# A planned kernel of retention and a two-layer PReLU network: scores and states of a pair of heads in one piece, and a planner that counts array switches and holds loads back

## The chip, the cores and the metric

The kernel runs on one NeuronCore of a Trainium2 chip: TensorE (PE) multiplies matrices, VectorE (DVE), ScalarE (ACT) and GpSimd (POOL) work elementwise, SyncE (SP) and ACT issue DMAs. Each engine runs its own instructions strictly in order and waits on semaphores for the others. The metric is the device time of one execution in microseconds (us), the median of several runs.

## The reference

Eight batches of eight heads, 576 positions, head size 64, all fp32. Each head computes a causal decayed product; the heads of a position are joined to a row of 512, and 4608 rows go through a layer of 2048 with a per-column PReLU and back to 512:

```python
scores = scale * np.matmul(q, k.transpose(0, 1, 3, 2))
gamma = 1.0 - 2.0 ** (-5.0 - np.arange(H, dtype=np.float32))
Dmat = np.where(rel >= 0, gamma[:, None, None] ** rel[None, :, :], 0.0)
attn = np.matmul(scores * Dmat, v)
x = attn.transpose(0, 2, 1, 3).reshape(B * S, H * D)
h = x @ w_in
out = (np.maximum(h, 0.0) + alpha * np.minimum(h, 0.0)) @ w_out
```

## The kernel before

**The retention.** The 64 heads are taken as 32 pairs (two heads of 64 rows fill 128 partitions). A sequence is cut into nine chunks of 64 positions. Within a chunk the masked scores are computed directly; across chunks a 64x64 state per head is carried, decayed and added to. Pairs 0 to 3 (the first batch) are done by separate functions at the start. For each later pair, `joint(n)` (it does one pair's scores and states and the values of the pair before) records:
- the values of pair n-1 (`values`, matmuls on line 758, 128x64 weights, 18 of them in two pieces, into the two PSUM banks psh), and ACT's copies of them to x (line 773);
- the corner scores of the ninth chunk (line 796, 2 matmuls of 64x64 weights into a corner of psh1);
- the scores of eight chunks (line 804, 16 matmuls of 64x64) and the states' increments (line 813, 16 of 64x64), in the two banks psa;
- DMAs of the scaled q to the tile at; masks of the scores (DVE lines 842 and 849; for pairs 4 to 7, called FIRST, ACT line 827 and POOL line 833);
- the running sum of the states (ACT 855 and 865, DVE 860, 868 and 871) and its DMAs into the tile vn, from which the next pair's values are computed.

Ahead of it `load_kq` loads q and k in a layout for transposing (tiles qx and kx, four DMAs of 72 KB each in packets of 128 bytes; each tile exists once) and k as it stands (kn, two DMAs of 144 KB in packets of 256 bytes). `operands` scales qx on POOL (line 730), transposes both on DVE (line 737, to kT and qT) and scales kn on ACT (line 742). `load_v` loads v. Pairs in FIRST load qx and kn from ACT's queue, all others from SP's.

The trace counts each of these fp32 matmuls twice (36, 4, 32 and 32 for a pair).

**The network.** 144 cells, each a block of 256 rows by a unit of 256 hidden columns. The first eight cells use fp32 matmuls (lines 951 and 981). The other 136 split each number into pieces: 24 matmuls of 128x256 on line 1015 into psh0 and psh1, an elementwise chain on ACT and DVE (lines 1023 to 1030), the split of the result on ACT and POOL (lines 1039 to 1046), and, two cells later, 12 matmuls of 128x512 on line 1064. Weights are loaded as raw words, converted (ACT 640 and 642, DVE 650 to 661, POOL 664) and split (ACT 688, POOL 689, DVE 692); half of them are kept in DRAM (wk) and read back. Finished x blocks and partial outputs are kept in DRAM too (xk, ok).

**What sets the order.** `do` (line 191) records each operation with an engine, a cost, and what it reads and writes. `plan` (line 224) first walks backwards to give every operation a due time (`due`, counted back from the end), then forwards: on each engine, among the ready operations that could begin within `SLACK` of the earliest one, the one with the smallest due time is next. A DMA occupies one model wire for size / `RATE`, and may be issued at most `BACKLOG` = 2 us ahead of that wire. The operations are then emitted in this order. No time of the plan is kept in the program: it is only the order that the plan decides.

Of the kernel before, what the change touches and what calls it, by code (L numbers as in the profile page):

```python
# [21 lines left out]
def kernel(  # L22
# [17 lines left out]
    C = 64  # L40
# [5 lines left out]
    TB = 2 * P  # L46
# [71 lines left out]
    for i in range(NBIT - 1):  # L118
# [8 lines left out]
                            op=ALU.mult)  # L127
# [60 lines left out]
                self.tile = self.slot.make()  # L188
            return self.tile

    def do(eng, cost, fn, r=(), w=(), late=0.0, lock=False):
        deps, gens = set(), []
        for keys, writes in ((r, False), (w, True)):
            for g, *sub in keys:
                wr, rd = g.keys.setdefault(tuple(sub), ([], []))
                deps.update(wr)
                if writes:
                    deps.update(rd)
                deps.update(g.before)
                if g not in gens:  # L200
                    gens.append(g)
        op = Op(eng, cost, fn, None, [g.slot for g in gens if g.slot and g.slot.bank], late, lock)
        for g, *sub in w:
            g.keys[tuple(sub)] = ([op], [])
        for g, *sub in r:
            g.keys[tuple(sub)][1].append(op)
        for g in gens:
            assert not g.slot or g.slot.gen is g
            g.ops.append(op)
        op.deps = [d for d in deps if d is not op]  # L210
        op.gens = gens
        ops.append(op)
        return op


    RATE = 220e3

    def dma(to, fro, size, r, w, eng="SP"):
        queue = {"SP": nc.sync, "ACT": nc.scalar}[eng]
        do(eng, 0.56, lambda: queue.dma_start(to(), fro()), r, w, late=size / RATE)  # L220

    LAT = {"PE": 0.2}

    def plan():

        users = [[] for _ in ops]
        for op in ops:
            for d in op.deps:
                users[d.n].append(op)

        def wait(d, op):
            return 2.0 if d.late else 0.0 if d.eng == op.eng else LAT.get(d.eng, 0.1)


        due = [0.0] * len(ops)
        left = [len(users[op.n]) for op in ops]
        can = [0.0] * len(ops)
        free = {e: 0.0 for e in BEGIN}
        ready = {e: [] for e in BEGIN}
        for op in ops:  # L240
            if not left[op.n]:
                ready[op.eng].append(op)
        for _ in ops:
            pick = None
            for e, queue in ready.items():
                if queue:
                    t0 = min(max(free[e], can[op.n]) for op in queue)
                    op = max((op for op in queue if max(free[e], can[op.n]) <= t0 + 0.02),
                             key=lambda op: op.n)
                    t = max(free[e], can[op.n])  # L250
                    if pick is None or t < pick[0]:
                        pick = t, op
            t, op = pick
            ready[op.eng].remove(op)
            free[op.eng] = t + op.cost
            due[op.n] = -(t + op.cost)
            for d in op.deps:
                left[d.n] -= 1
                can[d.n] = max(can[d.n], t + op.cost + wait(d, op) + d.late)
                if not left[d.n]:  # L260
                    ready[d.eng].append(d)
        left = [len(op.deps) for op in ops]
        ready = {e: [] for e in BEGIN}
        rest = [op.n for op in ops if op.eng == "PE"]
        end, begin, order = [0.0] * len(ops), [0.0] * len(ops), []
        free, held, port, wire = dict(BEGIN), {}, [0.0, ""], 0.0
        can = [0.0] * len(ops)
        for op in ops:
            if not op.deps:
                ready[op.eng].append(op)  # L270

        def earliest(op):
            t = max(free[op.eng], can[op.n])
            for b in op.banks:
                if b in held:
                    t = max(t, max([x + LAT.get(e, 0.1) for e, x in held[b].items()
                                    if e != op.eng] or [0.0]))
            if op.lock and port[1] != op.eng:
                t = max(t, port[0])
            if op.late:  # L280
                t = max(t, wire - BACKLOG)
            return t

        while len(order) < len(ops):
            pick = None
            for e, queue in ready.items():
                if not queue:
                    continue
                c = [(earliest(op), op) for op in queue
                     if e != "PE" or op.n <= rest[0] + AHEAD_PE]  # L290
                if not c:
                    continue
                t0 = min(t for t, _ in c)
                t, op = min((x for x in c if x[0] <= t0 + SLACK.get(e, 0.05)),
                            key=lambda x: (due[x[1].n], x[1].n))
                if pick is None or t < pick[0]:
                    pick = t, op
            t, op = pick
            ready[op.eng].remove(op)
            if op.eng == "PE":  # L300
                rest.remove(op.n)
            begin[op.n] = t
            free[op.eng] = t + op.cost
            end[op.n] = t + op.cost
            if op.late:
                wire = max(wire, t + op.cost) + op.late
                end[op.n] = wire
            for b in op.banks:
                held.setdefault(b, {})[op.eng] = t + op.cost
            if op.lock:  # L310
                if port[1] == op.eng or t + op.cost > port[0]:
                    port[:] = [t + op.cost, op.eng]
            order.append(op)
            for u in users[op.n]:
                left[u.n] -= 1
                can[u.n] = max(can[u.n], end[op.n] + wait(op, u))
                if not left[u.n]:
                    ready[u.eng].append(u)
        total = max(end)
        return total, order, begin, end  # L320

    AHEAD_PE = 150
    BACKLOG = 2.0
    LAG, FIRST = 2, range(4, 8)
    SLACK = {"PE": 0.02}
    BEGIN = {"PE": 5.0, "ACT": 0.5, "DVE": 8.2, "POOL": 5.8, "SP": 0.5}


# [368 lines left out]
    pairs = [(b, c) for b in range(B) for c in range(NPAIR)]  # L697
    loaded, turned, mts = {}, {}, {}
# [18 lines left out]
    def load_v(n):  # L717
        b, c = pairs[n]
        for h2 in range(2):
            dma(lambda h2=h2: vns[n % 2][half(1 - h2), h2],  # L720
                lambda h2=h2: v[b, 2 * c + h2].rearrange("(j t) d -> t j d", t=C), S * D * 4, (),
                [(vnm[n % 2], "v", h2)])
# [25 lines left out]
    def values(n, pv):  # L748
        b, c = pairs[n]
        vn, mt = loaded[n][3], mts[n]  # L750
        w = TB // C
        j1 = -b * NJ % w or w
        j1 += w if NJ - j1 > 6 else 0
        for i, js in enumerate((range(0, j1), range(j1, NJ))):
            def f(i=i, js=js):
                for j in js:
                    for h2 in range(2):
                        nc.tensor.matmul(pv[i].get()[half(h2), (j - js[0]) * C:(j - js[0] + 1) * C],  # L758
                                         vns[n % 2][:, h2, j], mt.get()[:, h2, j], start=True,
                                         stop=True)  # L760
            do("PE", 0.14 * len(js), f,
               [(vn, x, h2) for x in "vs" for h2 in range(2)] + [(mt, x, h2) for h2 in range(2)
                                                                for x in ("q", 0, 1, "x")],
               [(pv[i], 0)])
        j = 0
        while j < NJ:
            kb, o = divmod(b * NJ + j, w)
# [7 lines left out]
            do("ACT", 0.12 + 0.065 * m, f, [(pv[i], 0)], [(xb[kb], "c", c, j)])  # L775
            j += m

    def joint(n):
        pv = [Gen(psh[m]) for m in range(2)]
        if n - 1 in mts:  # L780
            values(n - 1, pv)
            if n + 1 < len(pairs):
                load_v(n + 1)
        if n == len(pairs):
            return
        c = pairs[n][1]
        kT, qT = turned[n]
# [6 lines left out]
        def f():  # L794
            for h2 in range(2):
                nc.tensor.matmul(pv[1].get()[half(1 - h2), 7 * C:], kT.get()[half(h2), chunk(NJ - 1)],
                                 qT.get()[half(h2), chunk(NJ - 1)], start=True, stop=True)
        do("PE", 0.15, f, [(kT, 0), (qT, 0)], [(pv[1], "x")])

        def f():  # L800
            for j in range(NJ - 1):
                for h2 in range(2):
# [1 line left out]
                    nc.tensor.matmul(at(j % 2)[x, 0, j // 2], kT.get()[half(h2), chunk(j)],  # L804
                                     qT.get()[half(h2), chunk(j)], start=True, stop=True,
                                     skip_group_check=True)
        do("PE", 0.65, f, [(kT, 0), (qT, 0)], [(ps[0], 0), (ps[1], 0)])

        def f():
            for j in range(NJ - 1):  # L810
                for h2 in range(2):
# [1 line left out]
                    nc.tensor.matmul(at(j % 2)[x, 1, j // 2], kn.get()[half(1 - h2), j],  # L813
                                     vns[n % 2][half(1 - h2), h2, j], start=True, stop=True,
                                     skip_group_check=True)
        do("PE", 0.65, f, [(kn, 0), (kn, 1), (vn, "v", 0), (vn, "v", 1)], [(ps[0], 1), (ps[1], 1)])
        mt = mts[n] = Gen(ats)
        for h2 in range(2):
            dma(lambda h2=h2: mt.get()[half(h2), h2].rearrange("p j s -> p (j s)"),
# [450 lines left out]
```

## Time and profile before

| | before |
|---|---|
| runs | median 979.19 us (978.96 to 982.37, 6 runs) |
| profiled execution | 979.08 us, span 977.4 us |
| granted TensorE clock, mean | 0.988 |
| a 128x256 group of a cell, L1015 x24 | 2.87 us |
| a 128x512 group of a cell, L1064 x12 | 2.75 us |
| L758, L804, L813, L796 busy | 40.1, 20.2, 19.5, 9.1 us |
| DMA | 134.93 MB, 255053 packets, 218448 under 512 B |
| kx, qx (SP), qx (ACT), kn (SP), kn (ACT): issue to landing, median | 3.2, 2.9, 6.0, 3.6, 5.2 us |

The profile is one execution, some 1.7 us longer than its span. Its views are: a page with the busy share of each engine, in all and in 40 slices; the same by stages given in us, with the granted clock and the DMA share; the chain of work that ended last, followed back through what released each step; and the instructions of an engine in order of time, where a bracket tells how long the engine had been idle and what ended that. Matmuls are pipelined, so durations of single ones overlap; what counts is the distance from start to start.

### The profile page before, as it was taken

How to read it: one execution, taken by the hardware profiler on the slowest of the kernel's cores; microseconds unless marked ns; L12 is line 12 of the kernel's file. 1: busy time of each engine (PE TensorE's matmuls, PEld its weight loads, DVE VectorE, ACT ScalarE, POOL GpSimd, SP SyncE). 2: the span in 40 equal slices, each digit the busy share in tenths (PEclk: the TensorE clock that was granted, in tenths of full speed). 3: DMA queues.
4: the chain of work that ended last, by engine and by line, in shares of the span. 5: the costliest groups of instructions: out<-in, count | busy, mean ns of one | idle time of the engine just before them, and what ended most of it. 6: DMA issues, size and time to landing. Idle time of an engine off the chain costs nothing.

```text
span 977.4 us, 22758 instructions
## 1 busy us (share of the span) xinstructions
PE 937.8 (96%) x8713; PEld 821.5 (84%) x8713; DVE 616.2 (63%) x1294; ACT 583.8 (60%) x1313; POOL 637.1 (65%) x515
## 2 busy tenths in 40 slices
PE   4897789999999999999999999999999999999998
PEld 4665468888998888888889899999999999999996
DVE  5776766778666777787667777554554445444444
ACT  3575455757666657576678676665555555555542
POOL 3766665766775848567688889765555555665553
PEclk9899899999999999999999999999999999999999
DMA  9989787888665979887533536242122212121111
GB/s 235 201 169 225 141 197 161 204 183 202 178 142 135 209 148 216 187 211 190 175 130 130 172 103 186 91 150 66 65 76 72 91 65 66 67 86 44 44 45 65
DMA packets 255053, 134.93 MB, mean 138 GB/s; under 512 B 218448, under 2 KB 218464, under 8 KB 254944
## 3 DMA queue, kind: packets, MB, share of 16 engines
q1 hardware_dynamic: 238624, 130.59, 52.0%
q10 hardware_dynamic: 16320, 2.89, 2.0%
q8 instruction: 68, 1.11, 0.5%
q14 instruction: 41, 0.34, 0.1%
HBM read 82.19 MB, written 35.65 MB: 121 GB/s over the span
## 4 chain that ended last, share of the span: by engine, by line
PE 83%; DMA 7%; SPq 3%; DVE 2%; POOL 2%; ACT 1%; issue 1%; ACTq 0%; POOLq 0%; DVEq 0%
PE psh L1015 38%; PE pso L1064 36%; PE psh L758 3%; SPq L220 3%; DMA vn<-su 2%; PE psh L951 1%; PE psa L804 1%; DMA kn<-in_k_dram 1%; PE psa L813 1%; PE pso L981 1%; DMA at<-qT 1%; DMA w<-in_q_dram 1%; DMA kx<-in_k_dram 1%; DMA qx<-in_q_dram 1%; DMA w<-in_k_dram 1%
## 5 line engine op out<-in xcount | busy, mean ns | idle before, releaser
L1015 PEld LDWEIGHTS psh<-lx,w 128*128 128x128 f32 x3264 | 409.6, 191 | 13.9 <-DVE ga L1030 2.0
L1015 PE MATMUL psh<-lx,w 128*128 128x256 f32 x3264 | 419.0, 284 | 0.2
L1064 PE MATMUL pso<-w,g 128*128 128x512 f32 x1632 | 402.9, 393 | 1.0 <-POOL g L1046 1.0
L1064 PEld LDWEIGHTS pso<-w,g 128*128 128x128 f32 x1632 | 295.8, 188 | 58.0 <-POOL g L1046 2.1
L1043 POOL TENSOR_TENSOR g<-ga,g 128x512 fp32r<-128x512 f32 x136 | 180.0, 1324 | 232.7 <-ACT g L1039 232.4
L1024 DVE SCALAR_TENSOR_TENSOR ga<-psh,gt 128x256 f32<-128x256 f32 x272 | 114.5, 422 | 172.8 <-ACT gt L1023 167.3
L1046 POOL TENSOR_TENSOR g<-g 128x512 fp32r<-128x512 f32 x136 | 178.5, 1313 | 12.0 <-ACT g L1041 2.0
L1030 DVE SCALAR_TENSOR_TENSOR ga<-psh,malpha,ga 128x256 f32<-128x256 f32 x272 | 130.2, 480 | 68.0 <-ACT psh L1027 66.9
L1039 ACT ACTIVATE g<-ga 128x512 fp32r<-128x512 f32 x136 | 85.9, 631 | 121.2 <-PE pso L1064 104.3
L1027 ACT ACTIVATE psh<-ga 128x256 f32<-128x256 f32 x272 | 105.2, 388 | 88.4 <-DVE ga L1024 87.0
L1023 ACT COPY gt<-psh 128x256 f32<-128x256 f32 x272 | 101.0, 371 | 66.5 <-PE psh L1015 58.9
L934 POOL TENSOR_TENSOR lx<-lx 128x512 fp32r<-128x512 f32 x78 | 102.3, 1322 | 18.8 <-DVE lx L924 16.2
L1041 ACT ACTIVATE g<-ga 128x512 fp32r<-128x512 f32 x136 | 84.4, 620 | 0.0
L842 DVE SCALAR_TENSOR_TENSOR at<-psa,pf,mask 64x256 f32<-64x256 f32 x96 | 46.3, 483 | 17.8 <-PE psh L758 7.0
L758 PEld LDWEIGHTS psh<-at,vn 128*64 128x64 f32 x1008 | 34.9, 143 | 20.5 <-issue 13.0
L730 POOL TENSOR_TENSOR qx<-qx,tabx 128x576 f32<-128x576 f32 x28 | 32.4, 1158 | 28.7 <-DMA qx<-in_q_dram 19.8
L758 PE MATMUL psh<-at,vn 128*64 128x64 f32 x1008 | 40.1, 232 | 10.9 <-DVE ga L962 7.0
L917 ACT ACTIVATE lx<-x 128x512 fp32r<-128x512 f32 x78 | 48.7, 628 | 0.0
L931 POOL TENSOR_TENSOR lx<-x,lx 128x512 fp32r<-128x512 f32 x30 | 38.8, 1294 | 3.7 <-ACT lx L929 3.7
L1082 DVE TENSOR_TENSOR op<-pso,op 128x512 f32<-128x512 f32 x46 | 31.6, 686 | 14.2 <-PE pso L1064 14.2
L773 ACT COPY x<-psh 128x256 f32<-128x256 f32 (+3 forms) x84 | 23.7, 320 | 18.3 <-PE psh L758 12.2
L924 DVE TENSOR_TENSOR lx<-x,psa 128x512 fp32r<-128x512 f32 x48 | 32.6, 679 | 2.1 <-PE psh L1015 1.9
(173 smaller groups left out, 848.7 us busy)
## 6 DMA issues: line engine op xcount, KB each, us to landing
ok<-o SPq DMA_DIRECT2D x48, 256.0 KB, 2.9
op<-ok SPq DMA_DIRECT2D x24, 512.0 KB, 3.9
x<-xk SPq DMA_DIRECT2D x23, 512.0 KB, 3.4
xk<-x SPq DMA_DIRECT2D x18, 512.0 KB, 4.8
out_dram<-o SPq DMA_DIRECT2D x36, 256.0 KB, 2.4
kx<-in_k_dram SPq DMA_DIRECT2D x112, 72.0 KB, 3.2
vn<-in_v_dram SPq DMA_DIRECT2D x56, 144.0 KB, 3.4
at<-qT SPq DMA_DIRECT2D x56, 144.0 KB, 3.3
```

What stands on the lines that cost most here:

```text
L758: nc.tensor.matmul(pv[i].get()[half(h2), (j - js[0]) * C:(j - js[0] + 1) * C], vns[n % 2][:, h2, j], mt.get()[:, h2, j], start=True, stop= ...
L934: do("POOL", 1.29, lambda c=c: nc.gpsimd.tensor_tensor(out=piece(to.get()[:, 2, c]), in0=to.get()[:, 0, c], in1=to.get()[:, 1, c], op=ALU. ...
L1015: nc.tensor.matmul(at(b), piece(w[:, l, c0:c0 + P]), piece(x.get()[:, l, cc]), start=(n == 0 and cc == 0), stop=(n > 0 and cc == NCC - 1), ...
L1023: do("ACT", 0.36, lambda t=t, at=at: nc.scalar.copy(t(), at(1)), [(ph, 1)], [(gt, f)])
L1024: do("DVE", 0.42, lambda t=t, g=g, at=at: nc.vector.scalar_tensor_tensor(out=g(), in0=at(0), scalar=ONE, in1=t(), op0=ALU.mult, op1=ALU.su ...
L1027: do("ACT", 0.39, lambda g=g, at=at: nc.scalar.activation(at(1), g(), ACTF.Relu, scale=-1.0), [(ga, f)], [(ph, 1)])
L1030: do("DVE", 0.48, lambda g=g, at=at, fc=fc: nc.vector.scalar_tensor_tensor(out=g(), in0=at(1), scalar=malpha[:, fc:fc + 1], in1=g(), op0=A ...
L1039: do("ACT", 0.64, lambda: nc.scalar.mul(piece(to.get()[:, 2]), ga.get(), BELOW), both, [(to, 2)])
L1041: do("ACT", 0.64, lambda: nc.scalar.mul(piece(to.get()[:, 0]), ga.get(), BELOW * 2.0 ** -12), both, [(to, 0)])
L1043: do("POOL", 1.29, lambda: nc.gpsimd.tensor_tensor(out=piece(to.get()[:, 1]), in0=ga.get(), in1=to.get()[:, 2], op=ALU.subtract), both + [ ...
L1046: do("POOL", 1.29, lambda: nc.gpsimd.tensor_tensor(out=piece(to.get()[:, 2]), in0=to.get()[:, 0], in1=to.get()[:, 1], op=ALU.subtract), [( ...
L1064: nc.tensor.matmul(a[2 * m + b].get(), piece(g.get()[:, l, f, m * P:(m + 1) * P]), piece(w_at[u, 2 + f].get()[:, l]), start=(cell["first"] ...
```

## The change

1. The four pieces of a pair on PE (values in two, corner, scores, states) are first collected. Pairs 8 and later record corner and scores as one operation; FIRST pairs keep them apart. The operations of the joint are recorded values first, and the copies of the values and the next `load_v` after them.
2. An operation can have a kind. Scores, states and corner have the kind "half" on PE, all else the kind of its engine; where the kind differs from the last operation's, the forward walk counts 0.12 us more. PE's SLACK goes from 0.02 to 0.14. The costs of the pieces are set lower (0.65 to 0.47, 0.15 to 0.03, 0.14 to 0.133 a chunk).
3. RATE goes from 220 to 236 (KB/ms, that is GB/s). RATE_256 and RATE_128 are defined and `dma` takes a rate.
4. A DMA isn't planned earlier than `HOLD` = 30 us ahead of its due time.

```diff
-    def do(eng, cost, fn, r=(), w=(), late=0.0, lock=False):
+    def do(eng, cost, fn, r=(), w=(), late=0.0, lock=False, kind=None):
...
-        op.gens = gens
+        op.gens, op.kind = gens, kind or eng
...
-    RATE = 220e3
-
-    def dma(to, fro, size, r, w, eng="SP"):
+    RATE, RATE_256, RATE_128 = 236e3, 175e3, 115e3
+
+    def dma(to, fro, size, r, w, eng="SP", rate=RATE):
         queue = {"SP": nc.sync, "ACT": nc.scalar}[eng]
-        do(eng, 0.56, lambda: queue.dma_start(to(), fro()), r, w, late=size / RATE)
+        do(eng, 0.56, lambda: queue.dma_start(to(), fro()), r, w, late=size / rate)
...
+        last = -min(due)
...
             if op.late:
-                t = max(t, wire - BACKLOG)
-            return t
+                t = max(t, wire - BACKLOG, due[op.n] + last - HOLD)
+            return t + SWITCH.get(op.eng, 0.0) * (kinds[op.eng] != op.kind)
...
-    BACKLOG = 2.0
+    BACKLOG, HOLD = 2.0, 30.0
     LAG, FIRST = 2, range(4, 8)
-    SLACK = {"PE": 0.02}
+    GROUPS = (("v0",), ("v1",), ("x", "s"), ("u",))
+    SLACK, SWITCH = {"PE": 0.14}, {"PE": 0.12}
...
+    def on_pe(parts, groups):
+        for some in groups:
+            do("PE", sum(parts[x][0] for x in some), lambda some=some: [parts[x][1]() for x in some],
+               [key for x in some for key in parts[x][2]],
+               [key for x in some for key in parts[x][3]], kind="half" if not {"v0", "v1"} & set(some) else None)
...
     def joint(n):
         pv = [Gen(psh[m]) for m in range(2)]
+        parts = {}
         if n - 1 in mts:
-            values(n - 1, pv)
-            if n + 1 < len(pairs):
-                load_v(n + 1)
+            (parts["v0"], parts["v1"]), rest = values(n - 1, pv)
         if n == len(pairs):
+            on_pe(parts, [["v0"], ["v1"]])
+            rest()
             return
...
-        do("PE", 0.15, f, [(kT, 0), (qT, 0)], [(pv[1], "x")])
+        parts["x"] = 0.03, f, [(kT, 0), (qT, 0)], [(pv[1], "x")]
...
+        groups = [["v0"], ["v1"], ["x"], ["s"], ["u"]] if n in FIRST else GROUPS
+        on_pe(parts, [[x for x in some if x in parts] for some in groups])
+        if n - 1 in mts:
+            rest()
+            if n + 1 < len(pairs):
+                load_v(n + 1)
```

More of the change, by code (lines that the diff above doesn't have):

```diff
@@ L265, in plan @@
         end, begin, order = [0.0] * len(ops), [0.0] * len(ops), []
-        free, held, port, wire = dict(BEGIN), {}, [0.0, ""], 0.0
+        free, held, port, wire, kinds = dict(BEGIN), {}, [0.0, ""], 0.0, {e: e for e in BEGIN}
         can = [0.0] * len(ops)
@@ L302, in plan @@
             begin[op.n] = t
-            free[op.eng] = t + op.cost
-            end[op.n] = t + op.cost
+            kinds[op.eng] = op.kind
+            free[op.eng] = end[op.n] = t + op.cost
             if op.late:
@@ L753, in values @@
         j1 += w if NJ - j1 > 6 else 0
+        parts = []
         for i, js in enumerate((range(0, j1), range(j1, NJ))):
@@ L760, in f, with keep_x @@
                                          stop=True)
[L761 to L764, printed above, removed]
+            parts.append((0.133 * len(js), f, [(vn, x, h2) for x in "vs" for h2 in range(2)] +
+                          [(mt, x, h2) for h2 in range(2) for x in ("q", 0, 1, "x")],
+                          [(pv[i], 0)]))
+        return parts, lambda: keep_x(n, pv, j1)
+    def keep_x(n, pv, j1):
+        b, c = pairs[n]
+        w = TB // C
         j = 0
@@ L806, in f @@
                                      skip_group_check=True)
-        do("PE", 0.65, f, [(kT, 0), (qT, 0)], [(ps[0], 0), (ps[1], 0)])
+        parts["s"] = 0.47, f, [(kT, 0), (qT, 0)], [(ps[0], 0), (ps[1], 0)]
         def f():
@@ L815, in f @@
                                      skip_group_check=True)
-        do("PE", 0.65, f, [(kn, 0), (kn, 1), (vn, "v", 0), (vn, "v", 1)], [(ps[0], 1), (ps[1], 1)])
+        parts["u"] = (0.47, f, [(kn, 0), (kn, 1), (vn, "v", 0), (vn, "v", 1)],
+                      [(ps[0], 1), (ps[1], 1)])
+        groups = [["v0"], ["v1"], ["x"], ["s"], ["u"]] if n in FIRST else GROUPS
[4 more added lines that the diff above has]
+                load_v(n + 1)
         mt = mts[n] = Gen(ats)
```

## The prediction

> **What bounds the kernel now.** I read the page's busy table and its 40 slices first, then the stages of 25 us, then the chain of work that ended last, then the engine timelines of the first 150 us. The page:
>
> ```profile
> PE 937.8 (96%) x8713; PEld 821.5 (84%) x8713; DVE 616.2 (63%) x1294; ACT 583.8 (60%) x1313; POOL 637.1 (65%) x515
> ...
> PE   4897789999999999999999999999999999999998
> ...
> DMA  9989787888665979887533536242122212121111
> ```
>
> TensorE is the bound from slice 7 on, and the DMA engines are full in the first four slices. The stages (columns: us, busy PE, PEld, DVE, ACT, POOL, granted clock, DMA share, GB/s) say the same with numbers:
>
> ```profile
> 0.00:25.00 25.00, 12.10 (x309) 10.31 (x310) 14.66 (x56) 9.01 (x14) 10.12 (x23) 0.94 1.08 235
> 75.00:100.00 25.00, 19.22 (x250) 13.20 (x248) 15.64 (x28) 13.18 (x29) 16.98 (x18) 0.93 1.01 208
> 100.00:125.00 25.00, 17.41 (x234) 12.30 (x236) 16.70 (x33) 10.86 (x24) 14.56 (x14) 0.86 0.74 148
> 125.00:150.00 25.00, 21.11 (x266) 17.51 (x259) 17.43 (x41) 12.81 (x32) 16.75 (x14) 0.93 0.88 210
> 250.00:275.00 25.00, 25.00 (x254) 22.35 (x255) 14.89 (x34) 16.42 (x38) 19.89 (x17) 1.00 0.60 138
> ```
>
> So two places can give time: the start-up to about 146 us, with some 33 us of idle PE, and the stage to 480 us, where PE never idles but interleaves the pairs' small matmuls with the full ones. After 480 us only full matmuls are left (2.87 + 2.75 us a cell), in an unchanged order: nothing to gain.
>
> What a small piece costs is read in the chain of work that ended last (start, us, what). First a joint cut in pieces, then one whose pieces stand together:
>
> ```profile
> 191.03 2.75 PE pso L1064 x12
> 193.77 0.62 PE psa L813 x32
> 194.40 0.10 PE psh L796 x4
> 194.50 1.59 PE pso L1064 x6
> 196.09 1.20 PE psh L758 x36
> 197.29 1.58 PE pso L1064 x6
> 198.88 2.87 PE psh L1015 x24
> 201.75 1.39 PE pso L1064 x6
> ```
>
> ```profile
> 255.38 1.20 PE psh L758 x36
> 256.58 0.20 PE psh L796 x2
> ...
> 257.30 0.47 PE psa L813 x32
> 257.77 3.06 PE psh L1015 x24
> ```
>
> Prices: going back to full matmuls costs 0.19 (1.58 or 1.59 against 1.39, 3.06 against 2.87), after values (L758) as after scores or states. Going in with scores or states costs 0.15 (0.62 against 0.47 when other small ones stand before). Going in with values is free (1.20 behind full and small alike). Values to the corner piece L796 costs 0.16 (0.26 in all, behind L813 only 0.10).
>
> **The change, part by part.** (1) Joining and the switch count. I counted, in the two built programs' PE order from the first split cell on, the runs of small matmuls between full ones. Before: 42 runs, 24 that begin with scores, states or corner, 20 steps from values to these. After: 40 runs, 13, and 24 (thirteen are now values, corner, scores, with or without states). So before 42 x 0.19 + 24 x 0.15 + 20 x 0.16 = 14.8 us, after 40 x 0.19 + 13 x 0.15 + 24 x 0.16 = 13.4: **-1.4 us**, all on the path, since PE never idles there. Bounds: the runs of before took 18.5 us in the chain above their bare work (1.20 + 0.10 + 0.47 + 0.47 a joint), 0.45 each. Two runs less at 0.45 are 0.9; and if the 18 of the 40 that hold values, corner and scores cost 0.34 (2.39 from 255.38 to 257.77, + 0.19 - 2.24) and the other 22 cost 0.45, 16.0 are left, a gain of 2.5.
>
> The Trainium skill, TensorEngine Tiling (Array Packing), Key Properties, says that any change of tiling mode drains the array. The 128x64 values would then be a mode of their own, which the planner's two kinds leave out; the row speaks against half of that, since entering values costs nothing. By the rule all 114 changes before and 108 after cost the same, and this term would be 6 x 0.19 = -1.1 instead.
>
> (2) The rates. No call passes RATE_256 or RATE_128: small packets aren't counted, and every transfer is counted faster than before (220 to 236 GB/s; 72 KB from 0.33 to 0.31 us). On the chip such loads take 2.9 us (SP) or 6.0 us (ACT) from issue to landing (median). It acts only through the order, so its price is in (3) and (4).
>
> (3) HOLD in the first 40 us. Before, ACT issues ahead of its first L688 (37.08 us) the four qx and two kn loads of pair 4 and two qx loads of pair 5: 6 x 72 + 2 x 144 = 720 KB. After, three qx loads stand ahead of it: 216 KB. That is 504 KB less while the DMA engines are full; at 213 GB/s, between the stages 0 to 25 (235) and 25 to 50 (192), it is 2.4 us. What it now holds up:
>
> ```profile
> 2.73 4.56 ACTq L220 DMA_DIRECT2D qx<-in_q_dram  x3
> 20.89 1.15 POOL L730 TENSOR_TENSOR qx<-qx,tabx 128x576 f32<-128x576 f32 x1 [8.91 <-DMA kn<-in_k_dram]
> ```
>
> ACT stands 4.56 us in three issues ahead of its first copy, and POOL's in-order queue stands 8.91 us at qx while the first weight piece (DVE done at 19.06) waits behind it to 21.99. Only 0.5 of that is PE's: its next need, ACT's x, ends at 22.82, PE starts at 23.33. The chain runs through DMA here (q 1.93 to 8.80, weights 8.82 to 13.66, k 29.88 to 35.60), so most of the 2.4 is on the path. I take **-1.9 us** (0 to -2.9, the 2.4 and the 0.5; nothing in this stage is moved ahead, so no loss).
>
> (4) The four joints of the start-up (60 to 146 us). PE idles there for 0.9 + 3.8 + 1.0 + 7.0 + 0.5 + 0.2 + 2.0 + 1.9 = 17 us. Three things change. Stores (ok0, xk0, xk1; 1.5 MB, 7 us of wire at 208 GB/s) go behind the next pair's loads and the states' copy: that copy takes 6.32 us from 71.00, against a median of 3.0, with ok0 issued 0.5 us ahead. Values now stand ahead of the next scores and states, so that DVE, which stood 3.7 us for them (L849 at 79.88, PE's values at 78.56), goes on earlier; L661 and POOL's L664, which end PE's 3.8 us wait, are behind it. And kx of pair 8 is now ahead of its qx: its transpose, waiting to 99.20 for that DMA, holds up the DVE queue in which L962 ends PE's 7.0 us wait. Against it: qx of pairs 5 to 7 are loaded one joint later, behind the transpose of the pair before. Their transposes stood 26.6, 15.6 and 18.1 us ahead of their scores (48.98, 73.96, 90.70 to 75.55, 90.32, 109.61). Now the chain from one transpose to the next is 6.0 (DMA) + 1.15 (L730) + 0.77 (L737) = 7.9 us, and the joints come 12.3 to 16 us apart: it fits, with 4 us or more to spare. Behind a late qT stand DVE's states and L962, and for these PE waits. The ends: -10.8 us (the 3.8 and the 7.0 both gone) and +9 (the three qT 3 us late each: the 4 spare spent by 7 us of waiting in ACT's, POOL's and DVE's queues). I take **-2.0**, near the wait that is surely shortened (the 3.3 of the slow copy) less a little for qx.
>
> TensorE: Matmul & The Clock Gate, Part 1, states that an idle window of some 3.4 us halves PE's clock until it has been busy as long. The trace agrees: after the 7.0 us wait the 36 value matmuls take 2.77 us (1.27 warm), and the granted clock is 0.86. If both long waits fell under that, the rule would add an estimated 2 x 1.7 = 3.4 us of gain, which the sum leaves out.
>
> (5) 146 to 480 us, transfers: DMA share 0.6 to 0.9, PE idles 1.4 us in all. The later qx and stores have that cover. If it is gone at one joint, a scores piece waits for a qx of 2.9 us: up to +2.9, within the range.
>
> Sum against the profiled execution: 979.08 us (span 977.4, 1.7 around it): 979.08 - 1.4 - 1.9 - 2.0 = 973.8. The median of the runs, 979.19, is 0.1 above; I keep **973.8**.
>
> **Rivals.** About 0.2% (2 us) is what a measurement of this kernel can tell from no change.
> A, the forecast: 970 to 976. For: DMA share 1.08 and 1.01 just where bytes are moved away. Chance 0.49.
> B, the waits merely move: PE's 17 us belong to a cycle (qx, transpose, scores, states, copy, values) that an earlier load at one point doesn't shorten, and only the 1.4 is left, with perhaps 0.3 of start-up: about 977.5 to 979. For: joints came every 12 to 16 us however their waits fell. Chance 0.17.
> C, slower: the single qx buffer is refilled one joint later, and qT comes late. It decides when load, scale and transpose take more than the 12.3 us between joints, which needs over 4 us of queueing beside the 7.9; ACT's DMA issues stand in order behind its copies. Price 3 joints x 3 us = 9, less the 1.4 and 1.9: 984.8. Against: the spare 4 us, and that POOL idles 8 of 25 us between 75 and 100. Chance 0.21.
> D, the long waits go: both of (4)'s, so 979.1 - 1.4 - 1.9 - 10.8 = 965.0, or with the 7.0 alone 968.8. For: both end at DVE's queue, which goes on earlier. Chance 0.13.
>
> **Numbers.** Faster by over 0.2%: A and D, 0.62; within: B, 0.17; slower: C, 0.21. The range holds A and B, most of D, and C up to half its price: 966 to 982.
>
> **What would show it.** Right: from 250 to 480 us nearly all runs are L758, L796, L804 together, and a joint costs some 0.06 us less (1.4 over 24); the second split cell starts near 142 instead of 146.2; POOL's 8.91 us at qx is gone; the wait of L758 for L962 is under 5 us. Wrong: new waits of DVE's L737 or POOL's L730 for qx between 60 and 130 us, or of L804 for L737, would be C; idle of some 17 us with other names, B; any PE idle after 480 us, for weights that are read back later, none of these.

## The result and the profile after

| | before | after |
|---|---|---|
| runs, same chip, taken together | median 980.76 us (977.68 to 987.64, 49 runs) | median 984.55 us (981.06 to 989.19, 24 runs) |
| ratio after to before | | **1.0036**, 95% interval 1.0024 to 1.0047 |
| profiled execution, span | 979.08, 977.4 us | 989.19, 987.5 us |
| the planner's own total for its order | 962.5 us | 953.9 us |

The changed kernel is **slower by 0.36%**, some 3.5 us; the forecast was 5.3 us faster. The planner believed in a gain of 8.6 us. The profiled execution of after is the longest of its runs, 4.6 us above its median, so the two profiles lie 10.1 us apart where the medians lie 3.8 apart: the profiles show where the time went, the runs how much.

The page of after, busy time and the slices of TensorE and of the DMA engines:

```profile
PE 941.0 (95%) x8713; PEld 824.4 (83%) x8713; DVE 617.8 (63%) x1294; ACT 582.5 (59%) x1313; POOL 632.9 (64%) x515
...
PE   4897889999999999999899999999999999999998
...
DMA  9897877687587786887436545242112222112111
```

The same work on every engine, and no fuller DMA. One slice after the start-up, the 20th (469 to 494 us), is no longer a 9. The stages (us, busy PE, PEld, DVE, ACT, POOL, granted clock, DMA share, GB/s):

```profile
0.00:25.00 25.00, 11.84 (x309) 10.17 (x310) 13.58 (x56) 9.25 (x15) 9.32 (x22) 0.89 1.06 248
75.00:100.00 25.00, 18.25 (x229) 13.18 (x224) 17.25 (x34) 13.44 (x30) 17.01 (x17) 0.86 0.76 162
100.00:125.00 25.00, 20.65 (x247) 12.24 (x247) 20.19 (x33) 11.93 (x26) 17.29 (x16) 0.93 0.82 183
125.00:150.00 25.00, 21.04 (x230) 18.07 (x228) 16.05 (x37) 11.95 (x31) 15.53 (x13) 0.86 0.72 152
475.00:500.00 25.00, 22.07 (x163) 19.67 (x162) 13.49 (x31) 16.79 (x39) 17.06 (x14) 0.93 0.42 141
```

From 75 to 150 us TensorE is a little busier than before (59.9 against 57.7 us), and between 75 and 100 the DMA share fell from 1.01 to 0.76: loads did move away. To put a place to the loss I use the start of the split cells, which are the same 136 pieces of work in every kernel (24 matmuls of L1015, now L1038). Cells 4 to 72 hold the same matmuls in both kernels, and from cell 72 to the end every kernel but one (after_packets below, 371.6) takes 370.4 to 370.8 us.

| start of split cell | before | after | difference |
|---|---|---|---|
| 4 | 159.16 | 157.66 | -1.5 |
| 32 | 350.46 | 349.25 | -1.2 |
| 44 | 437.92 | 440.16 | +2.2 |
| 52 | 494.18 | 502.37 | +8.2 |
| 72 | 606.89 | 617.01 | +10.1 |
| 4 to 72 | 447.74 | 459.35 | **+11.6** |

So the start-up gained 1.5, and the stage that I had called covered lost 11.6. TensorE's waits between 146 and 610 us (total, times, longest), first in before:

```profile
PE pso L1064 <- POOL g L1046: 0.6, 1, 0.6
PE psh L758 <- DMA vn<-su: 0.2, 1, 0.2
PE psh L796 <- DVE ga L1030: 0.2, 1, 0.2
```

and in after:

```profile
PE psh L761 <- DVE ga L1053: 2.6, 2, 2.2
PE psh L1038 <- DVE ga L1053: 2.4, 5, 1.2
PE psh L1038 <- ACT x L780: 2.2, 2, 1.3
PE psh L1038 <- POOL lx L957: 1.5, 1, 1.5
PE psa L829 <- DMA vn<-in_v_dram: 0.8, 1, 0.8
PE psh L761 <- DMA vn<-su: 0.6, 1, 0.6
```

1.0 us has become 10.1: 9.1 of the 11.6 are waits of TensorE that weren't there. They have no single owner: DVE, ACT, POOL and DMA end them in turn. Followed back, some end at a transfer and at an in-order queue behind it. The chain of work that ends the 2.2 us wait at 164.28 (start, us, what):

```profile
157.69 3.05 DMA vn<-su
160.74 0.01 issue
160.75 0.04 ACT kn L744
160.80 0.64 issue
161.44 0.61 ACT g L1062
162.05 0.52 ACT g L1064
162.57 0.27 ACT gt L1046
...
163.74 0.49 DVE ga L1053
164.23 0.04 issue
164.28 0.92 PE psh L761 x24
```

ACT's in-order queue stands at the scaling of kn (L744) until 160.75. The chain names the copy of the states for it (vn<-su), but L744 reads kn alone, and the second kn load of this pair, issued at 155.55, takes 5.2 us to land, that is until 160.7: ACT stands for that load. The cell's own three operations (g, g, gt) are queued behind it, DVE behind those, and TensorE's values behind DVE. Another wait ends directly at a load:

```profile
363.54 6.98 DMA vn<-in_v_dram
370.53 0.14 issue
370.66 0.81 PE psa L829 x30
```

The planner counts 2.6 us for this load (2.0 and 144 KB at 236 GB/s); here it took 7.0. Such loads are hardly slower than before in general (median 3.8 us against 3.4), and their users stand no closer behind them in general either: from the landing of a pair's v loads to its first matmul of the states it is 6.6 us in before and 6.9 in after (medians of 28 pairs). So this is one late load that met its user. Other waits stand behind work in a queue: in the chain, the 1.3 us ahead of 359.08 and the 1.2 us ahead of 557.97 follow the conversion of a late weight (wa), on DVE and on POOL.

### The profile page after: what moved, and what is told of

It reads as the page before. It is cut to its first block, busy times and chain, and to the rows that moved or that the text cites. A ratio compares the mean times of both kernels' runs of the same rounds, so it can differ in the third digit from the quotient of the medians.

```text
span 987.5 us, 22765 instructions
## 1 busy us (share of the span) xinstructions
PE 941.0 (95%) x8713; PEld 824.4 (83%) x8713; DVE 617.8 (63%) x1294; ACT 582.5 (59%) x1313; POOL 632.9 (64%) x515
## 4 chain that ended last, share of the span: by engine, by line
PE 80%; DMA 5%; DVE 4%; SPq 3%; ACT 3%; issue 2%; POOL 2%; POOLq 0%; ACTq 0%; DVEq 0%
PE psh L1038 35%; PE pso L1087 33%; SPq L220 3%; PE psh L761 3%; PE psh L974 2%; DMA vn<-su 2%; PE pso L1004 2%; PE psa L829 1%; DMA vn<-in_v_dram 1%; PE psa L820 1%; DMA kn<-in_k_dram 1%; DMA w<-in_q_dram 1%; DVE ga L1053 1%; PE psh L812 1%; DMA op<-in_moe_w_in_dram 1%
## 5 line engine op out<-in xcount | busy, mean ns | idle before, releaser
L1038 PEld LDWEIGHTS psh<-lx,w 128*128 128x128 f32 x3264 | 413.6, 193 | 20.8 <-DVE ga L1053 4.5
L1038 PE MATMUL psh<-lx,w 128*128 128x256 f32 x3264 | 423.6, 285 | 6.2 <-DVE ga L1053 2.4
L1066 POOL TENSOR_TENSOR g<-ga,g 128x512 fp32r<-128x512 f32 x136 | 177.8, 1307 | 242.0 <-ACT g L1062 234.3
L744 ACT ACTIVATE kn<-kn,tabk 128x576 f32<-128x576 f32 x28 | 21.7, 776 | 20.5 <-DMA kn<-in_k_dram 13.2
```

The lines of the kernel that those rows point to most:

```text
L1038: nc.tensor.matmul(at(b), piece(w[:, l, c0:c0 + P]), piece(x.get()[:, l, cc]), start=(n == 0 and cc == 0), stop=(n > 0 and cc == NCC - 1), ...
L1066: do("POOL", 1.29, lambda: nc.gpsimd.tensor_tensor(out=piece(to.get()[:, 1]), in0=ga.get(), in1=to.get()[:, 2], op=ALU.subtract), both + [ ...
```

## The experiments

Eighteen kernels, each timed in three rounds (3 to 10 executions in all) beside the kernel before. "Hold", "joining" and "rate" are the parts of the change: HOLD = 30; the collected pieces with their new costs, groups, SLACK 0.14 and SWITCH 0.12; RATE 236 (or 235). Cell 4 is when split cell 4 starts, 4 to 72 the time between these cells, both from one profiled execution each, so with some us of scatter; "plan" is the planner's own total.

| kernel | hold | joining | rate | ratio to before, 95% | cell 4 | 4 to 72 | plan |
|---|---|---|---|---|---|---|---|
| before | | | 220 | 1 | 159.2 | 447.7 | 962.5 |
| rate221 | | | 221 | 1.0050 (1.0033 to 1.0067) | 159.6 | 451.7 | 961.0 |
| lat21 | | | 220 | 1.0036 (1.0020 to 1.0052) | 161.6 | 453.3 | 963.4 |
| hold_only | x | | 220 | **0.9960** (0.9928 to 0.9992) | 150.8 | 451.4 | 951.4 |
| hold_221 | x | | 221 | **0.9895** (0.9869 to 0.9921) | 148.1 | 453.6 | 957.5 |
| hold_lat21 | x | | 220 | **0.9897** (0.9872 to 0.9922) | 150.6 | 451.7 | 954.3 |
| join_only | | x | 220 | 1.0035 (1.0012 to 1.0057) | 159.5 | 453.1 | 962.4 |
| rate_only | | | 236 | 1.0092 (1.0065 to 1.0118) | 157.7 | 455.8 | 955.4 |
| no_hold | | x | 236 | 0.9996 (0.9970 to 1.0022) | 158.9 | 455.3 | 953.0 |
| hold_rate | x | | 236 | 1.0036 (1.0017 to 1.0055) | 156.4 | 453.3 | 954.3 |
| hold_rate235 | x | | 235 | 1.0040 (1.0016 to 1.0065) | 155.5 | 456.3 | 959.9 |
| hold_join | x | x | 220 | 1.0009 (0.9988 to 1.0029) | 152.2 | 461.0 | 958.5 |
| hold_join221 | x | x | 221 | 0.9993 (0.9967 to 1.0018) | 149.6 | 457.1 | 957.4 |
| hold_unjoined | x | part | 220 | 0.9996 (0.9976 to 1.0016) | 150.0 | 457.5 | 957.2 |
| hold_joined_free | x | part | 220 | 1.0013 (0.9987 to 1.0040) | 153.7 | 456.4 | 952.1 |
| hold_apart_free | x | part | 220 | 1.0045 (1.0022 to 1.0069) | 152.8 | 463.0 | 949.4 |
| after | x | x | 236 | 1.0036 (1.0024 to 1.0047) | 157.7 | 459.4 | 953.9 |
| after_235 | x | x | 235 | 0.9972 (0.9943 to 1.0001) | 152.2 | 456.5 | 953.3 |
| after_packets | x | x | 236, 175, 115 | 1.0080 (1.0050 to 1.0111) | 153.6 | 462.9 | 975.1 |
| hold_packets | x | | 220, 175, 115 | 1.0097 (1.0074 to 1.0120) | 164.6 | 457.9 | 976.6 |

**First, one part off or one part on.** My theory after the profile was H: the hold moves the late weights' work (the first store to wk from 171.9 to 259.0 us, the read-backs to 527 to 618) into the stage that lost. Rivals: the joined order (J), the faster count of transfers (R).

`no_hold`: after, with

```diff
-    BACKLOG, HOLD = 2.0, 30.0
+    BACKLOG, HOLD = 2.0, 1e9
```

> The changed kernel with HOLD at 1e9 us, so that no DMA is planned later for its due time; joining, switch count, slack and rate stay. Theory H (holding back loads is the loss: the late weights' conversions start at 259 us instead of 172, and meet the pairs' last work and the read-backs between 440 and 620 us): the loss goes, ratio to before 0.996 to 1.000, and idle of PE after 146 us is under 3 us. Theory J (the joined order is the loss: values stand right ahead of a cell, which then waits for their copies): ratio stays 1.003 or more, with waits of the cells' first matmuls for ACT x. Theory R (the rate): no opinion here.

`join_only`: as no_hold, and

```diff
-    RATE, RATE_256, RATE_128 = 236e3, 175e3, 115e3
+    RATE, RATE_256, RATE_128 = 220e3, 175e3, 115e3
```

> The changed kernel without HOLD and with the rate of before: joining, switch count and slack alone. H: 0.997 to 1.000 (the runs of small matmuls priced as in the prediction are 13.9 us against 14.8). J: 1.003 or more. R: less than no_hold's ratio if the rate hurts.

`hold_only`: before, with

```diff
+        last = -min(due)
...
-                t = max(t, wire - BACKLOG)
+                t = max(t, wire - BACKLOG, due[op.n] + last - HOLD)
...
-    BACKLOG = 2.0
+    BACKLOG, HOLD = 2.0, 30.0
```

> The kernel before with HOLD = 30 us alone. H: 1.003 to 1.008, first store of a converted weight after 230 us, PE idle of 5 us or more after 400 us. J: 0.999 to 1.001. R: the same as J.

`rate_only`: before, with `RATE = 236e3`.

> The kernel before with the rate of 236 instead of 220 alone. H and J: 0.999 to 1.002 (46 runs of small matmuls, 15.2 us of switching against 14.8). R (a wire counted too fast makes loads late): 1.003 or more, with PE waiting for DMA or for DVE's transposes before 480 us.

Measured: 0.9996, 1.0035, 0.9960, 1.0092. Theory H fell. The hold by itself makes the kernel faster, although it moves the late weights just as far (first store 254.0 us, read-backs 521 to 603). Joining and rate each cost something alone, but together without the hold they cost nothing, so their prices don't add up.

**Second, the missing pairs and two edits without a meaning.** If prices don't add up, perhaps any edit deals a new order, good or bad. `hold_join` is after with RATE 220, `hold_rate` is hold_only with RATE 236. `rate221` is before with `RATE = 221e3`, `lat21` before with `LAT = {"PE": 0.21}` in place of 0.2.

> The changed kernel with the transfer rate put back to 220 GB/s: joining, switch price, slack and hold stay. Theory 'parts' (each part has a price of its own: hold -0.40%, joining +0.35%, rate +0.92%, as measured one by one): 0.9995 of the time before, and the second split cell starts some 8 us earlier than before, as with the hold alone. Theory 'rate' (the rate counted too fast is what costs the changed kernel its gain): as fast as the hold alone, 0.994 to 0.998. Theory 'order' (each edit gives another order, and an order's time scatters by half a per cent whatever the edit means): anywhere from 0.993 to 1.007, and not the product.

> The kernel before with the hold and with the rate of 236 GB/s, nothing joined. 'Parts': 0.996 x 1.0092 = 1.005. 'Rate': 1.003 or more. 'Order': anywhere from 0.993 to 1.009; a value under 1.000 would contradict both others.

> The kernel before with 221 GB/s in place of 220, a step that says nothing about the chip (72 KB counted 0.0015 us shorter) but gives the planner other ties. 'Parts' and 'rate': 0.999 to 1.001 (a sixteenth of 0.92% is 0.06%). 'Order': off by 0.3% or more either way in this or in the next kernel, with waits of TensorE at other joints.

> The kernel before with the planner's latency behind TensorE at 0.21 us in place of 0.20, again a step without a meaning of its own. 'Parts' and 'rate': 0.999 to 1.001. 'Order': off by 0.3% or more in this or in the kernel ahead.

Measured: 1.0009, 1.0036, 1.0050, 1.0036. Two edits that say nothing about the chip cost as much as the whole change. Between cells 4 and 72 they take 451.7 and 453.3 us against 447.7 of before: the order of before is a better one there than its two nearest neighbours, and every other kernel run here takes at least 451.4. The neighbours are the level which an edit should be held against: by it the changed kernel is no slower at all, and joining alone (1.0035) costs nothing that can be seen.

**Third, is the hold's gain real?** `hold_221` and `hold_lat21` are the two nudges with the hold added. `after_packets` and `hold_packets` hand in the two rates that the change defines and never uses:

```diff
-                    "ACT" if n in FIRST and g is qx else "SP")
+                    "ACT" if n in FIRST and g is qx else "SP", RATE_128)
...
-                [(vnm[n % 2], "v", h2)])
+                [(vnm[n % 2], "v", h2)], "SP", RATE_256)
```

and RATE_256 for kn likewise, in after and in hold_only.

> The hold added to the kernel before with 221 GB/s (which ran at 1.005 without the hold). Theory 'hold gains in the start-up' : 0.3 to 0.6% under its own partner, so 0.999 to 1.002, with the split cell 4 starting 3 to 8 us earlier than the 159.6 us of the partner. Theory 'order' (the 0.996 of the hold was one lucky order): no such distance; 1.003 to 1.009 is as likely.

> The hold added to the kernel before with 0.21 us of latency behind TensorE (1.0036 without the hold). 'Hold gains': 0.998 to 1.001, cell 4 starts 3 to 8 us before the partner's 161.6 us. 'Order': anywhere from 0.996 to 1.009. If both this and the last gain against their partners, the hold's gain is real and the changed kernel lost it elsewhere.

> The changed kernel with its two unused rates handed in: kx and qx at 115 GB/s, kn and v at 175, as its words say, all else at 236. The planner's own total rises from 953.9 to 975.1 us. Theory 'the plan counts transfers too fast' (the chip starts split cell 64 25 to 32 us behind the plan at 236 GB/s, 13 to 24 us behind at 220 GB/s): the distance shrinks to under 15 us, so cell 64 starts before 576 us and the time is 978 to 990, ratio 0.996 to 1.004, below that of the changed kernel by 0.2% or more if the distance falls under 8. Theory 'order': ratio anywhere from 0.996 to 1.009; the distance shrinks as well, since the plan is merely stretched.

> The kernel before with the hold and with the rates of small packets handed in (115 and 175, all else at 220), nothing joined. The planner's total is 976.6 us. 'The plan counts transfers too fast': cell 64 starts less than 8 us behind the plan's 561.9, ratio 0.994 to 1.000. 'Order': 0.996 to 1.009, and no better than the kernel ahead. Against the kernel ahead it tells what joining is worth under the same counting: by the price of a switch 1 to 2 us in its favour or none.

Measured: 0.9895, 0.9897, 1.0080, 1.0097. **The hold gains**, by 1.4 to 1.5% against its own neighbours and by 0.4 to 1.05% against before. (The spans of the three kernels are alike, 972.8, 972.1 and 972.8 us; the ratios differ partly because before ran at 982.8 us on one chip and 985.2 on the other. hold_221 rests on four executions, hold_lat21 on three. By the bare medians, 974.4 against 986.4 us and 974.5 against 985.7, the gain against the neighbours is 1.1 to 1.2%.) It gains where the prediction looked for it, and more: split cell 4 starts 8.4 to 11.1 us earlier. The stages of hold_221, to be compared with those of after above:

```profile
75.00:100.00 25.00, 17.84 (x151) 11.46 (x150) 20.73 (x40) 13.59 (x29) 19.56 (x19) 0.92 0.94 200
100.00:125.00 25.00, 21.72 (x280) 13.80 (x279) 15.30 (x33) 12.56 (x28) 18.16 (x16) 0.91 0.76 173
125.00:150.00 25.00, 24.43 (x307) 22.20 (x307) 18.34 (x44) 13.26 (x34) 14.22 (x12) 0.97 0.82 178
```

and TensorE's waits from 60 to 146 us in it:

```profile
PE psa L805 <- ACT lx L918: 3.3, 1, 3.3
PE pso L982 <- DVE ga L963: 3.0, 1, 3.0
PE psh L952 <- POOL g L665: 3.0, 1, 3.0
PE psh L797 <- DVE at L850: 0.8, 1, 0.8
PE psh L759 <- DVE ga L1031: 0.6, 2, 0.4
PE psh L759 <- DVE ga L963: 0.2, 1, 0.2
```

Together 10.9 us, against 17.2 in before and 15.6 in after. Counting the small packets at 115 and 175 GB/s was no help: the chip did stay nearer to the plan (span less plan 13.0 and 16.5 us, against 33.6 in after), as both theories said, but the plan itself is 21 us longer than that of after, and the time is 0.4% above after's. A plan that is nearer to the chip was not a better order.

**Fourth, do joining and rate lose as such?** `hold_join221` (after with 221), `hold_rate235` (hold_only with 235) and `after_235` are neighbours of the three kernels that have the hold and not its gain. `hold_joined_free` is hold_join with

```diff
-    SLACK, SWITCH = {"PE": 0.14}, {"PE": 0.12}
+    SLACK, SWITCH = {"PE": 0.02}, {"PE": 0.0}
```

> Hold and joining with 221 GB/s: the neighbour of the kernel that ran at 1.0009 with 220. Theory 'joining gives the gain of the hold back' : 0.998 to 1.004, with split cell 4 early by 6 us or more and the lead gone between 150 and 560 us. Theory 'one bad order' (the hold's partner with joining was an unlucky draw): at or under 0.993, like the hold at 221 GB/s without joining (0.9895).

> Hold and 235 GB/s, nothing joined: the neighbour of the kernel that ran at 1.0036 with 236. Theory 'the faster count costs the start-up' : 0.999 to 1.006, with split cell 4 at 154 us or later (148 to 151 with the hold at 220 and 221) and waits of the scores for DVE's qT or for the copied states between 100 and 135 us. 'One bad order': at or under 0.993, cell 4 at 148 to 152.

> The changed kernel with 235 in place of 236 GB/s. Theory 'joining and the faster count cost it': 1.000 to 1.007, cell 64 at 566 us or later. 'One bad order': 0.988 to 0.997.

> Hold and the joined piece at 220 GB/s, but the planner counts no switch (0 in place of 0.12) and lets no work of TensorE wait for a more urgent piece (slack 0.02 in place of 0.14). Theory 'the slack and the switch price of joining lose': 0.990 to 0.996, as the hold alone. Theory 'the joined piece itself loses' (scores and corner as one piece need free banks and operands at one time, and each joint has fewer pieces to fill gaps with): 0.999 to 1.004.

Measured: 0.9993, 1.0040, 0.9972, 1.0013. Joining and rate give the hold's gain back in neighbours too: three kernels with the hold alone lie at 0.9895 to 0.9960, the nine kernels with hold and joining or rate (220 to 236 GB/s) at 0.9972 or above. The interval of hold_only (up to 0.9992) still overlaps those of five of the nine; those of hold_221 and hold_lat21 (up to 0.9922) lie below all nine. The bare medians part as well: 974.4 to 977.9 us against 980.6 to 986.8. 0.9972 for after_235 is what neither theory expected: 1 GB/s less in the planner moves the changed kernel by 0.64%, and most of that is in the start-up (cell 4 at 152.2 instead of 157.7).

What the rate does in the start-up is plainest in hold_rate. POOL's in-order queue, then DVE's, then TensorE's (idle time and what ended it in brackets):

```profile
121.88 1.15 POOL L731 TENSOR_TENSOR qx<-qx,tabx 128x576 f32<-128x576 f32 x1 [9.29 <-DMA qx<-in_q_dram]
```

```profile
123.06 0.78 DVE L738 STREAM_TRANSPOSE qT<-qx 128x576 f32<-128x576 f32 x1 [2.45 <-POOL qx L731]
```

```profile
115.13 1.07 PE L805 MATMUL psa<-qT,kT 64*64 64x64 f32 x32 [2.29 <-DVE qT L738]
...
128.95 1.14 PE L805 MATMUL psa<-qT,kT 64*64 64x64 f32 x32 [5.96 <-DVE su L872]
```

The single qx buffer is refilled late (the first SP load of qx is issued at 97.7 us, in hold_221 at 86.8), POOL stands 9.3 us for the next one, and the transpose, the masks and the running sum of the states follow late. That is the chain that rival C describes. In after the same first load is issued at 100.6 us, in after_235 at 88.3.

**Fifth, which part of the joining?** The joined piece needs the values' second PSUM bank beside the two of the scores, so I suspected it. `hold_unjoined` is hold_join, `hold_apart_free` is hold_joined_free, each with

```diff
-    GROUPS = (("v0",), ("v1",), ("x", "s"), ("u",))
+    GROUPS = (("v0",), ("v1",), ("x",), ("s",), ("u",))
```

What is joined is the corner and the scores; the states, which the title names beside the scores, stay a piece of their own (`("u",)`) in every version.

> Hold and joining at 220 GB/s (1.0009), but with corner and scores left as two pieces; switch price, slack and the new costs of the pieces stay. Theory 'the joined piece loses' (scores need the values' second bank as well once the corner is in their piece): 0.988 to 0.997, the level of the hold without joining, and split cell 64 at 554 to 560 us instead of 568. Theory 'the switch price, the slack or the new costs lose': 0.999 to 1.004.

> The same edit in the kernel without switch price and slack (1.0013 with the joined piece): corner and scores as two pieces, new costs of the pieces. 'The joined piece loses': 0.988 to 0.997. 'The new costs of the pieces lose' (they are all that is left of the joining here, with the place of the values' copies and of the next v load in the list): 0.999 to 1.004.

Measured: 0.9996 and 1.0045, no better than with the joined piece (1.0009, 1.0013). That theory fell as well. What all five kernels with hold and some joining at 220 or 221 have in common is the rest of it: the lower costs of the pieces (a pair with corner counted at 2.17 us in place of 2.71; the forecast's prices make it 2.24 bare, and 2.59 with the switches of one joined run), and the place of the values' copies and the next v load in the list. These two were not tried one by one. A wait of hold_unjoined shows what a late spot looks like (chain, start, us, what):

```profile
530.93 0.42 DVE ga L1047
531.35 1.03 DVE wa L652
532.38 0.02 issue
532.40 1.41 DVE wa L654
...
534.45 0.49 DVE ga L1053
534.93 0.04 issue
534.98 1.69 PE psh L1038 x12
```

The conversion of a late weight (wa) stands in DVE's queue between the two operations of the cell, and TensorE waits for the second one, 1.7 us.

## Why the prediction was wrong, step by step

The step that failed is (5), the cover between 146 and 480 us, and with it the premise of (1) that PE never idles there. The sum has nothing for it, and the range 2.9 us; in the profile of after (its longest run; by the medians all in all 3.8 us are lost) the stretch between cells 4 and 72 is 11.6 us longer, and 9.1 of these are waits. Step (4) failed as well: none of its 2.0 us came.

- **(1) Joining and the switch count, -1.4.** The order came out as counted: 40 runs of small matmuls, 13 and 24 in the trace too (the runs of values, corner and scores are 18, as the bounds of the working have it, not thirteen). And a joined joint costs what the prices said. The timeline of after:

```profile
274.45 1.27 PE L761 MATMUL psh<-at,vn 128*64 128x64 f32 x36
275.65 0.27 PE L812 MATMUL psh<-qT,kT 64*64 64x64 f32 x2
...
276.23 0.68 PE L829 MATMUL psa<-vn,kn 64*64 64x64 f32 x31
276.85 3.13 PE L1038 MATMUL psh<-lx,w 128*128 128x256 f32 x24
```

  From the values' start to the next full matmul 2.40 us: 2.24 of bare work and the priced 0.16 from values to the corner. But a joint's saving is tenths, and the order that came with it has waits of whole microseconds. Without its waits, the stretch from cell 4 to cell 72 takes 446.7 us in before and 449.2 in after (447.74 less 1.0, 459.35 less 10.1); 1.7 of these 2.5 us can be put to the clock (below), and 0.8 more than before is left where the forecast has 1.4 less. Less waits and clock, the stretch takes 446 to 448 us in the ten kernels without joining and 447 to 451 in the ten with some of it, so the 1.4 is seen in none. What failed is "all on the path, since PE never idles there": that was true of the order of before, not of the next one.
- **(2) The rates, "it acts only through the order".** Right, but I priced it at nothing of its own in (3) and (4). On top of the hold it moved cell 4 from 148 to 151 us to 155.5 and 156.4, and the time from at most 0.9960 to 1.0036 and 1.0040.
- **(3) and (4) The hold in the start-up, -1.9 and -2.0.** Right in sign and place, and too small for the hold alone (8.4 to 11.1 us at cell 4, as far as D's 10.8). POOL no longer stands 8.91 us at qx, and the 7.0 us wait for DVE's L962 became 3.7. In the changed kernel (3) came: the matmuls of L951 (now L974) that began at 66.29 us begin at 64.08, 2.2 us earlier. But only 1.5 us arrive at cell 4, so (4) brought a loss of 0.7 in place of the gain of 2.0: the 3.8 us wait for POOL's conversion grew to 4.9, and the states stand 2.5 us for a v load that they had not waited for. (An early wait of L535, now L537, grew from 3.3 to 4.2; the 2.2 us are what is left with it.)
- **(5) "146 to 480 us, transfers: covered, at one joint up to +2.9".** Here the forecast broke: +11.6 in the profile between cells 4 and 72. I took the cover of before (1.0 us of waits in the 464 us from 146 to 610; the 1.4 us of idle PE in the working reach to 610 as well, to 480 it is 0.75) for a property of the work. It is a property of one order: the two kernels with a meaningless edit lose 4.0 and 5.5 us there, and those with the hold alone 3.7 to 5.8. "After 480 us nothing to gain" left out that something can be lost; I named idle there as "none of these" and gave it no chance.
- **Rivals.** C had the right sign and a time 0.25 us from the result, and its mechanism is what hold_rate shows; in after itself the wait for qT is 0.4 us, and the loss lies elsewhere. So C was not the cause of this result, and its time was right by luck. B's sign is the one that the start-up of after shows, 15.6 us of waits, in part under other names, against 17.2; but B expected no loss behind the start-up.

What is shown: the hold gains, joining and rate give it back, and orders next to each other differ by up to 0.6%. What stays open: which of the remaining parts of the joining does it, and why: that it is the pieces counted shorter than the chip runs them is only argued.

Of the versions run, the hold alone beats both kernels: 0.9960, 0.9895 and 0.9897 in three orders.

## What to carry to other kernels

Where a planner writes the order, an edit of its costs is a new deal of the whole order: run two or three edits without a meaning first, and take an edit's gain against their level, not against one order that may have been a lucky one. A planner's own total is no forecast (here it ranks after 8.6 us ahead of before, and hold_apart_free, the best plan of all, is one of the slower kernels). Idle time that is nearly nil in a profile tells how well this order fits, not how much slack the work has.

## What the runs showed of the hardware

Waits of TensorE of some 2 us can halve its clock for the 3.4 us that follow. In after the waits that end at 484.11, 487.73 and 490.24 us are 0.90, 0.49 and 1.53 us long; the stages of 3 us from there on (the clock is the number after the engines):

```profile
489.00:492.00 3.00, 1.76 (x9) 1.76 (x10) 0.48 (x1) 2.45 (x5) 3.00 (x3) 0.75 0.59 175
492.00:495.00 3.00, 3.00 (x16) 2.82 (x16) 1.32 (x3) 1.81 (x5) 2.92 (x3) 0.69 0.00 0
495.00:498.00 3.00, 3.00 (x20) 2.67 (x19) 0.50 (x2) 1.44 (x4) 2.84 (x4) 1.00 0.03 5
```

By stages of 1 us from 490 to 494 the clock is 0.74, 0.50, 0.50 and 0.55: half for some 3.4 us. So 2.9 us of waiting cost some 1.7 us more at the lower clock (0.25 and 0.31 of 3 us each). A single wait does it too, in hold_rate, where no other stands within 10 us ahead of it; the 24 matmuls behind it take 4.63 us, against 3.13 in the timeline of after above:

```profile
554.75 4.63 PE L1016 MATMUL psh<-lx,w 128*128 128x256 f32 x24 [1.73 <-DVE ga L1031]
```

```profile
555.00:558.00 3.00, 3.00 (x18) 3.00 (x18) 2.89 (x5) 1.43 (x4) 2.04 (x2) 0.59 0.27 88
```

Between 150 and 940 us the twenty profiles have eleven such drops, each behind 1.6 to 2.3 us of waits within 3.4 us. Not every such wait does it: 2.19 us up to 164.28 in after and 3.35 us up to 548.41 in hold_rate235 left the clock at 1.00. What decides it, no run here shows. The Trainium skill, TensorE: Matmul & The Clock Gate, Part 1, ties the drop, in its table of the two states, to an idle window of about 3.4 us; here waits well under that did it.
